# The opening of the first stage as one listed order for all engines

## The chip, the core and the metric

The kernel runs on one core of one Trainium2 chip. A core has five engines that take their instructions in order, each from a queue of its own: PE (TensorE, matrix products), ACT (ScalarE), DVE (VectorE), POOL (GpSimd) and SP (SyncE, which here only issues transfers). Sixteen DMA engines move data between HBM and the core. The metric is the device time of one execution in microseconds (us); a change is quoted against the kernel before.

## What is computed

```python
scores = q @ k.T / 8          # 4 sequences, 8 heads, 576 positions, head size 64
scores = where(0 <= i - j < 64, scores, -1e9)
x = softmax(scores) @ v       # joined over heads: 2304 tokens x 512
h = max(x @ w1, x @ w2, x @ w3)        # 512 -> 768
y = h @ w_out                          # 768 -> 512
h2 = y @ w_in                          # 512 -> 2048
g = where(h2 >= 1, h2, where(h2 <= -1, 0, (h2 + 1)**2 / 4))
out = g @ w_out2                       # 2048 -> 512
```

The weights arrive as 64-bit floats; q, k and v as 32-bit floats. Each big product is made of three passes over rounded "high" and "low" parts: high x high, high x low, low x high.

## The kernel before

**The first stage.** It interleaves the attention with the products of x with w1, w2 and w3. Attention is cut into 36 blocks `g` of 64 queries; two neighbouring blocks share one load of q and k. Tokens are cut into nine column blocks `j` of 256 (four attention blocks each). One *product* (`a_item`, 12 matmuls of 256 columns, line 423) multiplies one column block by one 128-column slice `f` of one of the three weights `w`; every column block takes 18 products. Products of blocks 0 and 1 are interleaved from the twelfth on (`LAG`), so in the order of issue the products A0 to A17 are fifteen of block 0 and three of block 1. After A17 come 144 more, and then two further stages (lines 766 and 993).

**An attention block, step by step.** `load` brings q and k (SP); `prep` transposes them on PE (line 296) and copies the results out of PSUM with ACT (`qt`, line 299) and DVE (`kring`, line 301); `qk` multiplies (PE, line 335); `red` takes the masked maximum (DVE, line 346); `ex` takes four exponentials (ACT, line 358); `norm` forms a reciprocal (DVE, lines 366 and 367) and scales the row (POOL, line 368); `ptr` transposes (PE, line 377); `ptc` copies out (line 385 on DVE for odd blocks below 8, else ACT); `pv` multiplies by v (PE, line 398); `val` writes the high part of x (ACT) and the low part (DVE, line 113).

**A weight pair, step by step.** The 18 weight slices are fetched and decoded as nine pairs of 1024 columns, pair n serving products 2n and 2n+1 of a column block. `w_load` issues two transfers of 512 KB into a staging buffer `wst`, of which there are three (`NW`). `w_word` decodes the upper and the lower words in place (two ACT instructions, lines 194 and 110). `w_shift` shifts the upper word into a tile `wt`, of which there are two (DVE, line 206). `w_add` adds the lower word (DVE, line 210). `w_high` rounds the sum into the arena (ACT, `arena<-wt`, line 110). `w_low` subtracts in two halves (POOL, line 113). So the five links are a chain: words, shift, add, high, low.

**What sets the order.** Steps are put at positions, a position being an index of a product, and sorted. `SEQ` (line 58) lists the steps of blocks 0 to 3 and three weight pairs ahead of the first product; blocks 4 to 7 lie at fixed distances from the products; a weight pair follows each product of column block 0. Up to position 12 (`visits[0]`) this is only the order in which steps are handed to a planner, which arranges each engine's queue by its own reckoning of times; from there on `chained` ties each step behind the ones before it on PE, ACT, DVE and SP. No tie makes one engine wait for another: it fixes the order in each queue.

**PSUM.** Products and the transposes of `prep` share one pool (`pmm`) of three buffers; a buffer comes free when its reader on ACT or DVE is done.

Of the kernel before, what the change touches and what calls it, by code (L numbers as in the profile page):

```python
# [58 lines left out]
    "L0 V1 P0 L2 V2 V3 Q0 Q1 E0 N0 E1 N1 P2 T0 Q2 X0 T1 Q3 E2 N2 E3 X1 N3 "  # L59
    "T2 X2 T3 X3 W3"  # L60
# [5 lines left out]
def kernel(ctx, tc, q, k, v, w1, w2, w3, wo1, wi2, wo2, out, hd, x2d, td, gd):  # L66
# [83 lines left out]
    queued = []  # L150

    def after_queued(fn, *args):
        with ExitStack() as stack:
            for i in queued:
                stack.enter_context(tc.issue_after(i))
            n = len(nc.cur_bb.bb.instructions)
            fn(*args)
        ends = [i for i in nc.cur_bb.bb.instructions[n:] if i.engine == mybir.EngineType.SP]
        queued[:] = ends[-1:] or queued

# [45 lines left out]
    def w_value(st):  # L212
        w_shift(st)
        w_add(st)

    def w_high(s, st):
        act_copy(s[:, 0], decoded[id(st)].bitcast(F32))

    def w_low(s, st):
        t = decoded.pop(id(st)).bitcast(F32)  # L220
        for x in (slice(0, 512), slice(512, 1024)):
            sub(nc.gpsimd, s[:, 1, x], t[:, x], f32(s[:, 0, x]))
# [18 lines left out]
    def load(g):  # L241
# [3 lines left out]
        if g in pet and g % 2 == 0:  # L245
            t = apool.tile([P, 2, 512], F32, tag="nat", name="nat", bufs=4)
            for x, src in enumerate((q, k)):
# [8 lines left out]
            nat[g // 2] = t  # L256
# [28 lines left out]

    def prep(g):
        b, i, s = blk(g)
        d = st_g[g]
        if g in pet:
            if g % 2:  # L290
                return
            qt = apool.tile([P, NP, 2, BL], F32, tag="qt2", name="qt2", bufs=2)
            for x in range(2):
                tp = pmm.tile([P, NP, P], F32, tag="mm", name="tp")
                for p in range(NP):
                    nc.tensor.transpose(tp[:, p, :], nat[g // 2][:, x, p * P:(p + 1) * P], ident)
                tp = tp.rearrange("a p (t c) -> a p t c", t=2)
                if x == 0:
                    act_copy(qt, tp)
                else:  # L300
                    nc.vector.tensor_copy(kring[:, :, s:s + 2, :], tp)
            for x in range(2):
                st_g[g + x]["q"] = qt[:, :, x, :]
# [76 lines left out]
    def ptc(g):  # L380
        d = st_g[g]
        W = d["W"]
        pt = apool.tile([P, NP, P], F32, tag="pt", name="pt", bufs=3)
        if g < 8 and g % 2:
            nc.vector.tensor_copy(pt[0:W], d["pps"][0:W])
        else:
            act_copy(pt[0:W], d["pps"][0:W])
        d["pt"] = pt
# [13 lines left out]
    def values(g, n, xt, off):  # L402
# [3 lines left out]
        act_copy(hl[0], o)  # L406
        sub(nc.vector, hl[1], o, f32(hl[0]))
# [9 lines left out]
    def a_item(j, f, w):  # L417
        t0, n = blocks1[j]
# [185 lines left out]
    def val(g, n=1):  # L604
        j, o = gblock[g]
        if o == 0:
            xt_new(j)
        values(g, n, xts[j], o)

    def pv_x(g):  # L610
        pv(g)
        val(g)

    def qk_r(g):
        qk(g)
        red(g)
# [8 lines left out]
    FS = (0, 3, 1, 4, 2, 5)  # L625
    order1 = [(w, f) for f in FS for w in range(3)]
# [443 lines left out]
```

## Time and profile before

| | us |
|---|---|
| median of 3 runs | 765.75 (765.6 to 770.11) |
| the profiled execution | 766.48 |
| its span, first to last instruction | 764.6 |
| PE busy | 738.2 (97%) |
| DVE, ACT, POOL busy | 574.2, 424.7, 261.9 |

The profiled execution is 0.73 us above the median, and 1.9 us of its time lie outside its span. Shares over the whole span say little about one stage: the page's 40 slices of 19.1 us each, and tables by stretch, show where PE isn't busy and at which clock it ran. A row of the timeline gives start, duration, engine, line, operation and tiles, with the idle time before it and what ended it in square brackets. A row of the groups gives the busy sum and the mean duration of one instruction.

### The profile page before, as it was taken

How to read it: one execution, taken by the hardware profiler on the slowest of the kernel's cores; microseconds unless marked ns; L12 is line 12 of the kernel's file. 1: busy time of each engine (PE TensorE's matmuls, PEld its weight loads, DVE VectorE, ACT ScalarE, POOL GpSimd, SP SyncE). 2: the span in 40 equal slices, each digit the busy share in tenths (PEclk: the TensorE clock that was granted, in tenths of full speed). 3: DMA queues.
4: the chain of work that ended last, by engine and by line, in shares of the span. 5: the costliest groups of instructions: out<-in, count | busy, mean ns of one | idle time of the engine just before them, and what ended most of it. 6: DMA issues, size and time to landing. Idle time of an engine off the chain costs nothing.

```text
span 764.6 us, 17458 instructions
## 1 busy us (share of the span) xinstructions
PE 738.2 (97%) x6680; PEld 718.2 (94%) x6680; DVE 574.2 (75%) x1313; ACT 424.7 (56%) x808; POOL 261.9 (34%) x315
## 2 busy tenths in 40 slices
PE   4798999999999999999999999999999999999997
PEld 3687989999999999999999999999999999999997
DVE  3697667777787884768876688777878999988881
ACT  5795575556565543535457767767675444443330
POOL 1647295355535462200048533731368000000000
PEclk9599999999999999999999999999999999999999
DMA  9977879896999975796778553555556545544421
GB/s 260 249 238 196 211 176 272 246 341 174 266 269 280 312 251 186 222 295 209 211 231 274 192 161 120 192 193 177 188 172 193 170 139 152 164 127 121 129 82 56
DMA packets 221651, 154.75 MB, mean 202 GB/s; under 512 B 95232, under 2 KB 213632, under 8 KB 221568
## 3 DMA queue, kind: packets, MB, share of 16 engines
q1 hardware_dynamic: 191600, 110.91, 52.0%
q10 hardware_dynamic: 26384, 28.06, 10.5%
q0 software_dynamic: 3584, 14.68, 4.9%
q8 instruction: 52, 0.85, 0.4%
q14 instruction: 31, 0.25, 0.1%
HBM read 98.24 MB, written 55.38 MB: 201 GB/s over the span
## 4 chain that ended last, share of the span: by engine, by line
PE 43%; DVE 3%; ACT 2%; DMA 1%; issue 1%; ACTq 0%; DVEq 0%
PE cc L766 6%; PE dz L993 6%; PE dx L993 6%; PE dy L993 6%; PE ce L766 6%; PE ca L766 6%; PE cb L766 3%; PE dw L993 3%; DVE plain L490 1%; DMA plain<-t_scratch 1%; ACT arena L110 1%; DVE side L113 1%; DMA plain<-g_scratch 1%; ACT ut L861 1%; DVE left L113 0%
## 5 line engine op out<-in xcount | busy, mean ns | idle before, releaser
L423 PE MATMUL ps<-xt,arena 128*128 128x256 f32 x1944 | 235.6, 281 | 5.0 <-ACT ht L110 1.7
L423 PEld LDWEIGHTS ps<-xt,arena 128*128 128x128 f32 x1944 | 229.5, 188 | 9.1 <-issue 2.0
L110 ACT ACTIVATE side<-plain 128x1024 fp32r<-128x1024 f32 (+3 forms) x64 | 61.6, 978 | 55.9 <-DVE plain L490 36.2
L110 ACT ACTIVATE arena<-plain 128x1024 fp32r<-128x1024 f32 (+3 forms) x62 | 60.0, 977 | 36.1 <-DVE plain L490 23.5
L490 DVE TENSOR_TENSOR plain<-plain 128x256 f32<-128x256 f32 (+1 forms) x172 | 76.3, 461 | 4.3 <-DMA plain<-g_scratch 1.9
L113 DVE TENSOR_TENSOR side<-plain,side 128x1024 fp32r<-128x1024 f32 (+3 forms) x53 | 60.8, 1172 | 17.7 <-ACT side L110 17.7
L113 POOL TENSOR_TENSOR arena<-plain,arena 128x256 fp32r<-128x256 f32 (+1 forms) x65 | 55.0, 879 | 47.3 <-ACT arena L110 47.2
L113 POOL TENSOR_TENSOR side<-plain,side 128x256 fp32r<-128x256 f32 (+1 forms) x38 | 34.6, 945 | 102.4 <-ACT side L110 83.6
L358 ACT ACTIVATE sm<-sm,nm 128x128 f32<-128x128 f32 (+1 forms) x144 | 55.3, 388 | 16.9 <-DVE nm L346 14.8
L110 ACT ACTIVATE ht<-ps 128x256 f32<-128x256 f32 x54 | 20.5, 382 | 79.2 <-PE ps L423 48.4
L368 POOL TENSOR_TENSOR sm<-sm,rs 128x512 f32<-128x512 f32 (+1 forms) x36 | 36.3, 1007 | 69.3 <-DVE rs L367 43.1
L490 DVE TENSOR_TENSOR hq<-hq 128x128 f32<-128x128 f32 x108 | 54.1, 502 | 1.6
L113 DVE TENSOR_TENSOR arena<-plain,arena 128x1024 fp32r<-128x1024 f32 (+3 forms) x34 | 40.7, 1202 | 6.0 <-ACT arena L110 5.8
L862 ACT ACTIVATE ut<-ut 128x288 f32<-128x288 f32 x64 | 43.9, 686 | 2.0
L436 DVE TENSOR_TENSOR ht<-ps,ht 128x256 f32<-128x256 f32 x54 | 22.7, 421 | 29.5 <-PE ps L423 14.9
L210 DVE CUSTOM_DVE_ANT_0 wt<-wst,wt 128x1024 uint16<-128x1024 uint16 (+1 forms) x47 | 42.1, 912 | 1.6 <-ACT wst L110 0.3
L871 DVE SCALAR_TENSOR_TENSOR ut<-ut,evt 128x864 f32<-128x864 f32 x32 | 38.3, 1196 | 1.6 <-ACT ut L862 1.6
L490 POOL TENSOR_TENSOR wx<-wt 128x256 f32<-128x256 f32 x26 | 19.3, 743 | 56.2 <-DVE wt L210 48.5
L436 DVE TENSOR_TENSOR hq<-ps,ht 128x256 f32<-128x256 f32 x54 | 22.5, 416 | 20.3 <-PE ps L423 17.4
L113 POOL TENSOR_TENSOR arena<-wt,arena 128x512 fp32r<-128x512 f32 (+1 forms) x26 | 33.9, 1330 | 9.0 <-ACT arena L110 8.9
L847 DVE TENSOR_TENSOR evt<-cc,evt 128x288 f32<-128x288 f32 x64 | 29.1, 455 | 8.8 <-PE cc L766 6.6
L110 ACT ACTIVATE evt<-ca 128x288 f32<-128x288 f32 x40 | 16.2, 406 | 34.0 <-PE ca L766 28.9
(164 smaller groups left out, 1775.9 us busy)
## 6 DMA issues: line engine op xcount, KB each, us to landing
g_scratch<-ut ACTq DMA_DIRECT2D x64, 288.0 KB, 3.0
plain<-g_scratch SPq DMA_DIRECT2D x36, 512.0 KB, 4.3
plain<-t_scratch SPq DMA_DIRECT2D x16, 896.0 KB, 5.2
h_scratch<-hq SPq DMA_DIRECT2D x27, 448.0 KB, 5.1
plain<-h_scratch SPq DMA_DIRECT2D x12, 1008.0 KB, 7.6
wst<-in_moe_w_out SPq DMA_DIRECT2D x22, 512.0 KB, 5.8
wst<-in_moe_w SPq DMA_DIRECT2D x18, 512.0 KB, 6.3
wst<-in_moe_w_in SPq DMA_DIRECT2D x16, 512.0 KB, 5.6
```

The lines of the kernel that those rows point to most:

```text
L110: nc.scalar.activation(dst, src, AF.Copy, scale=scale)
L113: eng.tensor_tensor(dst, a, b, op=ALU.subtract)
L210: nc.vector.tensor_tensor(t[:, x], t[:, x], st[:, x, 0], op=ALU.add)
L358: nc.scalar.activation(sm[:, p, 0:W], sm[:, p, 0:W], AF.Exp, bias=d["nm"][:, p:p + 1], scale=-1.0, accum_out=ss[:, p:p + 1])
L368: nc.gpsimd.tensor_tensor(sm[:, :, 0:W], sm[:, :, 0:W], rs.unsqueeze(2).to_broadcast([P, NP, W]), op=ALU.mult)
L423: nc.tensor.matmul(ps[:, 0:n], w_col((w, f), wl, kt), xt[:, xl, kt, 0:n], start=(x == 0), stop=(x == len(passes) - 1))
L436: nc.vector.tensor_tensor(t[:, 0:n], ps[:, 0:n], part[j, f][:, 0:n], op=ALU.max)
L490: eng.tensor_tensor(o, a, b, op=op)
L766: nc.tensor.matmul(o, wt.of(m, wl)[:, at * P:(at + 1) * P], wx.of(m, xl)[:, kt], start=start and x == 0, stop=x == len(passes) - 1, skip_g ...
L862: nc.scalar.activation(o, o, AF.Square)
L871: nc.vector.scalar_tensor_tensor(o, o, 2.0 ** WS, x, op0=ALU.min, op1=ALU.max)
L993: nc.tensor.matmul(o, quarter(gc[k % 4].hl[gl], RA[m])[:, r], wd[p].of(m, wl), start=bool(first and p == 0 and i == 0), stop=p == NPR - 1 ...
```

## The change

`SEQ` becomes one list of single steps up to the end of the eighteenth product, for all engines, the loads included. Each token is a step and a number: LQ, LK, LV, LW load q, k, v and a weight pair; TQ, TK and CQ, CK are the transposes and the copies of `prep`; QK, R, E as before, R and E in halves a and b; S is the reciprocal and N the scaling; PT, PC, PV as before; VH and VL the two parts of x; A the twelve matmuls of a product and D its read-out; H and ST sums and store of h; W1., W0., SH, AD, HI, LO the links of a weight pair. A star puts a copy on DVE (for CK: on ACT). Tokens without `@` stand ahead of A0; `@x` is a position.

All steps are now tied from the start, and POOL's too up to position 12. Blocks 4 to 7, and the steps of blocks 8 and 9 up to their scaling, leave the loops and stand in the list. The weight chain is rewired: the lower word is decoded into `wt` (`w_lower`), the upper word is shifted in place in `wst` (`w_upper`), `w_sum` adds them, and `w_high` rounds the shifted upper word alone, so that it no longer needs the sum. HI0, HI3 and HI8 run on DVE, the others on ACT. No instruction is added or left out; copies change engine and order. One step far behind, the last of eight steps on the second loaded chunk of the third stage, moves from position 31.58 to 31.05.

```diff
 SEQ = (
-    "L0 V1 P0 L2 V2 V3 Q0 Q1 E0 N0 E1 N1 P2 T0 Q2 X0 T1 Q3 E2 N2 E3 X1 N3 "
-    "T2 X2 T3 X3 W3"
+    "LQ0 LK0 TQ0 LQ1 CQ0 TK0 LK1 *CK0 TQ1 QK0 LK2 CQ1 QK1 R0a LQ2 TK1 E0a R0b R1a E0b TK2 LW0 CK1 E1a TQ2 S0 QK2 R1b "
+    "N0 CQ2 QK3 E1b R2a PT0 E2a R2b LV1 CK2 E2b *PC0 LV2 QK4 W0.0 S1 PV0 S2 LW1 N1 W1.0 R4a R3a N2 PT1 E3a R3b R4b "
+    "QK5 E3b SH0 E4b PT2 S3 LV3 *HI0 W0.1 AD0 LV4 W1.1 LQ3 *PC1 LO0a E4a *PC2 PV1 LK3 VH0 SH1 TQ3 N3 R5a LV5 HI1 TK3 "
+    "R5b LO0b S4 LW2 PT3 VH1 VL0 E5a VL1 PV2 N4 *PC3 CQ3 *CK3 AD1 PT4 VH2 E5b QK6 LQ4 VL2 LO1a W1.2 S5 PV3 R6a LW3 "
+    "W0.2 N5 TQ4 R6b QK7 E6a SH2 PT5 CQ4 LO1b R7a HI2 R7b LV6 AD2 E7a LW4 VH3 LO2a W1.3 VL3 "
+    "A0@0 E6b@0.19 SH3@0.33 E7b@0.74 LO2b@0.83 S6@0.9 A1@1 LW5@1.26 D0@1.29 S7@1.45 W1.4@1.56 N6@1.73 A2@2 PC4@2.33 "
+    "*HI3@2.47 W0.3@2.75 D1@2.98 N7@2.98 A3@3 D2@3.25 W0.4@3.3 LV7@3.3 AD3@3.42 PT6@3.58 W1.5@3.74 PV4@3.77 SH4@3.92 "
+    "A4@4 LW6@4.01 D3@4.32 *PC5@4.36 LO3a@4.36 PC6@4.59 A5@5 HI4@5.01 SH5@5.2 AD4@5.57 HI5@5.68 PT7@5.75 A6@6 "
+    "*PC7@6.21 LO3b@6.21 W1.6@6.23 LW7@6.31 D4@6.55 PV5@6.72 LO4a@6.86 D5@6.88 D6@6.92 A7@7 VH5@7.28 W0.5@7.55 "
+    "H5a@7.71 A8@8 LO4b@8.12 D7@8.24 LK4@8.25 W1.7@8.43 VL5@8.49 AD5@8.88 A9@9 W0.6@9.04 H5b@9.32 VH4@9.37 LW8@9.38 "
+    "TK4@9.44 D8@9.51 LO5a@9.51 D9@9.56 VL4@9.64 *CK4@9.71 PV6@9.83 SH6@9.91 A10@10 VH6@10.2 LO5b@10.2 HI6@10.4 "
+    "VL6@10.5 PV7@10.72 AD6@10.85 W1.8@10.94 A11@11 D10@11.36 W0.7@11.37 LO6a@11.43 QK8@11.54 D11@11.69 QK9@11.75 "
+    "VH7@11.78 R8a@11.89 A12@12 ST5@12 LO6b@12.01 VL7@12.1 E8a@12.24 R8b@12.39 E8b@12.84 SH7@12.9 A13@13 D12@13.39 "
+    "AD7@13.54 HI7@13.66 A14@14 H11a@14.4 D13@14.41 W0.8@14.68 LO7a@14.84 R9a@14.84 A15@15 R9b@15.29 E9a@15.44 "
+    "D14@15.6 LO7b@15.89 S8@15.9 E9b@15.98 A16@16 D15@16.28 H11b@16.79 A17@17 N8@17.23 D16@17.28 S9@17.58 SH8@17.96 "
+    "*HI8@17.98 AD8@17.98 D17@17.98 LO8a@17.98 LO8b@17.98 N9@17.98 ST11@18"
 )
...
+    def w_lower(st):
+        t = decoded[id(st)] = stg2.tile([P, 1024], I32, tag="wt", name="wt", bufs=WT)
+        act_copy(t, st[:, :, 0].bitcast(U32), scale=2.0 ** -29)
+
+    def w_upper(st):
+        w = st[:, :, 1]
+        nc.vector.tensor_scalar(w, w, 3, None, op0=ALU.logical_shift_left)
+
+    def w_sum(st):
+        t = decoded[id(st)]
+        nc.vector.tensor_tensor(t, t, st[:, :, 1], op=ALU.add)
+
+    def w_high(s, st, copy):
+        copy(s[:, 0], st[:, :, 1].bitcast(F32))
...
-    TIED = (mybir.EngineType.PE, mybir.EngineType.Activation, mybir.EngineType.DVE, mybir.EngineType.SP)
+    TIED = [mybir.EngineType.PE, mybir.EngineType.Activation, mybir.EngineType.DVE, mybir.EngineType.SP, mybir.EngineType.Pool]
     for at, _, fn, args in order:
         if fn:
-            chained(fn, *args, tie=at >= visits[0])
+            if at >= visits[0]:
+                TIED[4:] = ()
+            chained(fn, *args)
...
-                      (28.1, 28.11, 28.12, 28.13, 29.9, 30.05, 30.58, 31.58),
+                      (28.1, 28.11, 28.12, 28.13, 29.9, 30.05, 30.58, 31.05),
```

## Rows read from the trace of the kernel before

**Rows 1.** The page's slices of 19.1 us: PE's busy tenths and its granted clock.

```profile
PE   4798999999999999999999999999999999999997
PEclk9599999999999999999999999999999999999999
```

**Rows 2.** Table by stretch: length, then each engine's busy us; PEclk, DMA share, GB/s.

```profile
17.00:34.70 17.70, 11.68 (x104) 8.57 (x104) 12.86 (x35) 14.49 (x39) 11.08 (x9) 0.53 0.96 239
34.70:75.10 40.40, 36.64 (x381) 33.62 (x378) 33.68 (x88) 31.30 (x72) 23.91 (x17) 0.99 0.76 229
75.10:124.00 48.90, 47.83 (x517) 45.84 (x516) 32.55 (x111) 30.75 (x80) 27.72 (x34) 1.00 0.82 205
124.00:752.00 628.00, 624.59 (x5516) 615.80 (x5515) 486.76 (x1041) 339.70 (x594) 195.89 (x243) 1.00 0.66 201
```

**Rows 3.** Timeline: ACT's first copy, the first product, the eighteenth product's read-out.

```profile
5.14 0.60 ACT L110 ACTIVATE qt<-tp 128x512 f32<-128x512 f32 x1 [2.91 <-PE tp L296]
...
34.74 1.82 PEld L423 LDWEIGHTS ps<-xt,arena 128*128 128x128 f32 x13 [0.33 <-issue]
...
75.21 0.42 DVE L436 TENSOR_TENSOR hq<-ps,ht 128x256 f32<-128x256 f32 x1 [0.97 <-PE ps L423]
```

**Rows 4.** Waits from 0 to 80 us: total us, times, longest.

```profile
ACT arena L110 <- DVE wt L210: 7.8, 4, 4.2
PE ops L398 <- DVE xt L113: 5.6, 2, 4.3
...
PE ps L423 <- ACT ht L110: 1.7, 1, 1.7
```

**Rows 5.** Table by stretch again, one us each, around both changes of clock.

```profile
18.00:19.00 1.00, 0.00 (x0) 0.00 (x0) 1.00 (x3) 1.00 (x6) 0.00 (x0) 0.61 1.13 338
...
35.00:36.00 1.00, 1.00 (x8) 1.00 (x9) 1.00 (x8) 0.42 (x3) 0.59 (x1) 0.85 1.09 354
```

**Rows 6.** Groups by form, 0 to 73.7 us, ACT, DVE, POOL: busy us, mean ns.

```profile
L358 ACT ACTIVATE sm<-sm,nm 128x128 f32<-128x128 f32 x32 | 12.4, 390 | 2.8 <-DVE nm L346 1.5 <-POOL sm L368 1.4
L110 ACT ACTIVATE wst<-wst 128x1024 int32<-128x1024 uint32 x9 | 10.3, 1146 | 0.0
...
L110 ACT ACTIVATE arena<-wt 128x1024 fp32r<-128x1024 f32 x9 | 9.5, 1058 | 7.9 <-DVE wt L210 7.8
...
L110 ACT ACTIVATE qt<-tp 128x512 f32<-128x512 f32 x6 | 3.5, 587 | 2.9 <-PE tp L296 2.9
L110 ACT ACTIVATE xt<-ops 128x256 fp32r<-128x256 f32 x8 | 3.0, 370 | 0.0
...
L210 DVE CUSTOM_DVE_ANT_0 wt<-wst,wt 128x2048 uint16<-128x2048 uint16 x9 | 14.3, 1587 | 0.9 <-ACT wst L110 0.3
...
L113 POOL TENSOR_TENSOR arena<-wt,arena 128x512 fp32r<-128x512 f32 x18 | 27.8, 1568 | 9.0 <-ACT arena L110 8.9
```

**Rows 7.** Timeline of PE's weight loads, 76 to 89 us: one row for each kind.

```profile
76.31 0.87 PEld L377 LDWEIGHTS pps<-ident,sm 128*128 128x128 f32 x8
...
77.37 0.86 PEld L335 LDWEIGHTS sps<-kring,qt 64*64 64x64 f32 x32 [0.20 <-issue]
...
82.62 0.90 PEld L296 LDWEIGHTS tp<-ident,nat 128*128 128x128 f32 x8
...
83.48 4.27 PEld L423 LDWEIGHTS ps<-xt,arena 128*128 128x128 f32 x36
...
87.89 1.16 PEld L398 LDWEIGHTS ops<-pt,vr 128*64 128x64 f32 x32
```

**Rows 8.** Tile wst, 0 to 80 us: durations min/median/max in ns; landing of its transfers.

```profile
L206 DVE TENSOR_SCALAR wt<-wst x9: 681/694/1808, 16.2 to 64.0; 128x1024 int32<-128x1024 int32 x9
L210 DVE CUSTOM_DVE_ANT_0 wt<-wst,wt x9: 1216/1260/2300, 17.2 to 66.0; 128x2048 uint16<-128x2048 uint16 x9
...
DMA to landing us min/median/max: 3.5/6.3/10.0
```

**Rows 9.** Timeline of DVE: the step moved far behind.

```profile
577.04 1.52 DVE L113 TENSOR_TENSOR left<-plain,left 128x768 fp32r<-128x768 f32 x1
```

More of the change, by code (lines that the diff above doesn't have):

```diff
@@ L1 @@
+import re
 from collections import defaultdict
@@ L149 @@
     wslot = {}
[L150 to L159, printed above, removed]
     def w_load(pair, slot):
@@ L239, in natural, with load @@
         return g % 4 != 0
-    def load(g):
+    def load(g, half=(0, 1)):
         b, i, s = blk(g)
@@ L245, in load @@
         if g in pet and g % 2 == 0:
-            t = apool.tile([P, 2, 512], F32, tag="nat", name="nat", bufs=4)
-            for x, src in enumerate((q, k)):
+            if g // 2 not in nat:
+                nat[g // 2] = apool.tile([P, 2, 512], F32, tag="nat", name="nat", bufs=4)
+            t = nat[g // 2]
+            for x in half:
+                src = (q, k)[x]
                 for y in range(1) if i + 1 < NBB else range(2):
@@ L284, in vload, with prep_t, prep_c @@
         d["vr"] = t
+    def prep_t(g, x):
+        tp = st_g[g]["tp", x] = pmm.tile([P, NP, P], F32, tag="mm", name="tp")
+        for p in range(NP):
+            nc.tensor.transpose(tp[:, p, :], nat[g // 2][:, x, p * P:(p + 1) * P], ident)
+    def prep_c(g, x, copy):
+        tp = st_g[g]["tp", x].rearrange("a p (t c) -> a p t c", t=2)
+        if x == 0:
+            qt = apool.tile([P, NP, 2, BL], F32, tag="qt2", name="qt2", bufs=2)
+            copy(qt, tp)
+            for y in range(2):
+                st_g[g + y]["q"] = qt[:, :, y, :]
+        else:
+            copy(kring[:, :, blk(g)[2]:blk(g)[2] + 2, :], tp)
     def prep(g):
@@ L291, in prep @@
                 return
-            qt = apool.tile([P, NP, 2, BL], F32, tag="qt2", name="qt2", bufs=2)
             for x in range(2):
[L294 to L303, printed above, removed]
+                prep_t(g, x)
+                prep_c(g, x, (act_copy, nc.vector.tensor_copy)[x])
         else:
@@ L353, in ex @@
         W, sm = d["W"], d["sm"]
-        if pairs[0] == 0:
+        if "ss" not in d:
             d["ss"] = apool.tile([P, NP], F32, tag="ss", name="ss", bufs=5)
@@ L378, in ptr, with ptc @@
         d["pps"] = pps
-    def ptc(g):
+    def ptc(g, copy=act_copy):
         d = st_g[g]
@@ L383, in ptc @@
         pt = apool.tile([P, NP, P], F32, tag="pt", name="pt", bufs=3)
[L384 to L387, printed above, removed]
+        copy(pt[0:W], d["pps"][0:W])
         d["pt"] = pt
@@ L683 @@
+    for x, tok in enumerate(SEQ.split()):
+        tok, _, at = tok.partition("@")
+        for step in early(tok):
+            put(float(at or -100 + 0.01 * x), *step)
     g0 = blocks1[PB][0] // BL
```

131 lines of the change are left out of this document (61 added, 70 removed).

## Prediction, made before the changed kernel ran

> **What bounds the kernel now.** I read the page's slices first, to see where PE isn't full or not at its clock. From the third slice on PE is at nine tenths and the clock full; the first two slices are at four and seven tenths, with half the clock in the second [rows 1]. So whatever this change can give lies ahead of about 80 us. The table by stretch confirms it: from 124 to 752 us PE is busy 624.6 of 628 us, and just behind the eighteenth product 47.8 of 48.9 [rows 2]. What the opening saves should therefore reach the end, since the stretches behind it are bound by PE and move forward as a whole.
>
> Then the timeline, for two marks. The first product starts at 34.74. A17 ends at about 75.1, since its read-out on DVE starts at 75.21 released by PE [rows 3]. Up to A17 the list issues the same work as the kernel before (I counted each kind of step to that mark: five pairs of transposes plus block 10's, ten QK, eight PT, eight PV), so the gain of the opening is 75.1 less the new end of A17.
>
> The waits say who held whom. ACT waited 7.8 us in four waits for the sum on DVE before it could round a weight's high part: the link that the change takes out. PE waited once 4.3 us for the low part of x on DVE [rows 4]. [...]
>
> **What A0 costs to reach.** The list doesn't shorten the work ahead of A0; it even adds to it (E5 whole, halves of E6 and E7, QK6, QK7, PT4, PT5, the transposes of block 8). A0 needs VL3 on DVE, and that needs VH3 on ACT. ACT's share of the list ahead of and with VH3, by mean durations [rows 6]: 28 exponentials at 0.39 (10.9; block 0's are narrower, which I ignore), six word decodes at 1.15 (6.9), HI1 and HI2 at 1.06 (2.1), seven copies of transposes at 0.59 (4.1), four VH at 0.37 (1.5): 25.5 us. ACT's first copy starts at 5.14 [rows 3], so VH3 can't end before 30.6, and A0 not before 31. Walking the list step by step with these durations I find three waits that stay: ACT idles about 1.8 us ahead of 12 us, while the first loads, transposes and copies still follow one another; 1.0 at HI1, which stands behind SH1 and so behind AD0 on DVE; 0.4 at VH2, behind PV2. That gives 34.2: the first product starts where it did, not earlier. Bounds: 32 (two thirds of these 3.2 us gone) and 37 (the list's PE steps on the chain at half clock, some ten of them ahead of A0, each 0.3 longer).
>
> **What lies between A0 and A17.** Work that PE does there, from weight loads in the stage behind, at full clock [rows 7]: 18 products at 4.27/3 = 1.42 (25.6); PT6 and PT7 0.9; PV4 to PV7 2.3; QK8 and QK9 0.9; TK4 and the transposes of block 10 1.35; some three quarters of a us for switches at 0.1 to 0.2 each: 31.8. Before, the same stretch took 75.1 - 34.7 = 40.4, since it held 2.2 us more of attention on PE (two PT, two QK, half of a pair of transposes, at the same rows) and 3.8 us in which PE wasn't busy [rows 2]; the other 2.6 are short pieces between bursts, which the view counts as busy.
>
> Then the waits that the new order makes. (a) TK4 stands ahead of A10 on PE and needs LK4, which SP issues behind LW7; LW7 waits for the buffer that HI4 and AD4 free (my walk: 44.4), and behind load 10 (0.5 MB) come 1 MB and 0.25 MB, some 1.8 MB at the stretch's 229 GB/s [rows 2], 7.9 us: about 52 where PE comes to it at 51: 1.0 us. PV6, A10 and all later products are queued behind TK4. (b) The transposes of block 10 lie between A15 and A16, while D14 and D15 are listed behind them; with three PSUM buffers the second transpose must wait for the first copy and A16 for the second or for D15: two copies near 0.6 [rows 6], 1.3 us. (c) Weight pairs that come just in time (LO3 to LO5 end 0.3 to 3 us ahead of their product in the walk): 1.0 us. Sum 34.2 + 31.8 + 1.0 + 1.3 + 1.0 = 69.3. Unknown from the trace: whether (a) is 0 or, with the longest landing of 10.0 us instead of the median of 6.3 [rows 8], 5; I take 1.0, since the queue is as full as before.
>
> **The smaller edits.** Rounding high beside the sum removes ACT's 7.8 us of waits for DVE [rows 4] and costs nothing on DVE: shift and sum are the same instructions. Cover is lost at one place: the lower word now goes to one of two `wt` tiles, so ACT stands behind POOL's lows of two pairs before; in the walk they are 0.5 to 3 us early; where they aren't, the next exponentials and read-outs on ACT wait too. On POOL the list only orders lows and scalings, and POOL was busy 23.9 of 40.4 us [rows 2]; on SP it puts the first weight pair ahead of v, which ACT, full by then, doesn't see. The in-place shift and the HI copies on DVE have no row. Between 0.68, the shortest shift, and 1.81, the longest [rows 8], I take 1.0; DVE was free for 6.7 of 40.4 us behind A0 [rows 2], so both ends stay hidden there; not so HI0, which puts up to 0.8 us on A0's chain and is in its bounds. The spread 681 to 1808 ns comes where POOL's lows run beside the shift. [...]
>
> The step moved far behind: 1.52 us of DVE ahead of read-outs that PE waits for in tenths [rows 9]. Moved before them it can save or cost a few tenths; I count 0, with 0.5 to either side.
>
> **Sum.** 75.1 - 69.3 = 5.8 us. The profiled execution took 766.48, so 760.7; it stood 0.73 above the median of 765.75, so 760.0 for the median.
>
> **Rivals.**
> *The first half packs tighter.* If the list's order matches the chip, ACT's waits ahead of 12 us shrink and DVE's work overlaps: A0 at 32 and 0.7 us of waits behind it: 32 + 31.8 + 0.7 = 64.5, gain 10.6, 755.2. For it: ACT was busy only 14.5 of 17.7 us ahead of A0 and DVE 12.9 [rows 2]. Against it: ACT's 25.5 us can't start sooner.
> *The loads set the pace (slower side).* SP's queue is now one fixed order with three staging buffers; a weight load that waits for its buffer holds LK4, and so PE at TK4. If a pair comes every 4.5 us LK4 is in time within 1 us. From LK4 landing later than 57 the gain is gone; with landings near 10 us for three loads in a row (3 x 3.7 us late) it lands at 63, and A17 ends at 80.3: 771.0. For it: landings up to 10.0 us occurred [rows 8]. Against it: the median is 6.3, and the list starts loads as soon as the planner did.
> *The clock.* PE has done PT5 some 3 us before A0 in the walk, a gap near the one behind which the clock fell (4.3 us, [rows 4, 5]). [...] Against it: the gap is shorter than the one seen.
>
> **How the numbers follow.** About 1% (7.7 us) is what a measurement of this kernel can tell from no change. Forecast (a gain of 3 to 7.7): 0.45. Tighter packing (above 7.7): 0.30. The clock (1 to 3): 0.10. The loads: 0.15, of it 0.05 with landings later still (A17 behind 82.8, slower by over 1%) and 0.10 within. So faster 0.30, same 0.65, slower 0.05. The likeliest time is 760.0; its own range is 757 to 763. The range for 8 in 10 runs from 754 (A0 at 32, no waits: 63.8, 11.3 gained) to 767 (A0 at 37 with 6 us of waits: 74.8, or the milder cases of the loads).
>
> **What would show it.** [...] I am wrong in A0's term if it starts before 32 or after 37; in the waits if PE stands for over 2 us at `tp` for `nat<-in_k`, or at `ps`; and in the carry-over if A17 ends sooner and the span doesn't shrink by as much.

## The result, and the profile after

The changed kernel takes 772.83 us (770.35 to 774.74, seven runs) beside 765.75 for the kernel before (764.07 to 770.33): the ratio is 1.0056, with a 95% interval from 1.0029 to 1.0083. The two medians lie further apart, 0.92%; the median of the kernel before in four later sets of rounds was 767.35 to 768.93, so 765.75, from which the forecast starts, is a low one. Forecast were 760.0 and a range to 767. The profiled execution took 770.42, its span 768.6.

The page's slices of 19.1 us, PE's busy tenths and its granted clock, answer [rows 1]. PE is no busier in the first two slices together (5 and 6 tenths for 4 and 7), but its clock is higher in the second. The third slice is less full (8 for 9); the fourth is fuller (9 for 8) at a lower clock. The fourteenth, 249 to 268 us, stands at 8 where the kernel before has 9:

```profile
PE   5689999999999899999999999999999999999997
PEclk9798999999999999999999999999999999999999
```

The table by stretch answers [rows 2] (length, each engine's busy us, PEclk, DMA share, GB/s). Ahead of A0 the clock is now 0.80 and not 0.53; between A0 and A17 it is 0.88 and not 0.99, and that stretch has grown from 40.4 to 41.6 us:

```profile
17.00:34.40 17.40, 9.66 (x110) 7.38 (x108) 13.72 (x43) 14.31 (x42) 9.17 (x8) 0.80 1.10 265
34.40:76.00 41.60, 37.05 (x333) 34.71 (x334) 28.15 (x61) 26.62 (x54) 19.06 (x15) 0.88 0.66 193
...
124.00:752.00 628.00, 622.46 (x5491) 614.15 (x5490) 488.10 (x1042) 340.17 (x595) 195.88 (x244) 1.00 0.67 202
```

PE's timeline from 28 to 82 us shows where (start, length, line, operation, count, and in brackets the idle time ahead with what ended it; L285 transposes, L401 PV, L433 products):

```profile
34.43 7.72 PE L433 MATMUL ps<-xt,arena 128*128 128x256 f32 x48 [2.94 <-ACT xt L125]
...
48.63 4.51 PE L433 MATMUL ps<-xt,arena 128*128 128x256 f32 x36
55.32 1.09 PE L285 MATMUL tp<-ident,nat 128*128 128x128 f32 x4 [2.18 <-DMA nat<-in_k]
57.20 1.12 PE L401 MATMUL ops<-pt,vr 128*64 128x64 f32 x16 [0.80 <-DVE xt L128]
58.25 2.93 PE L433 MATMUL ps<-xt,arena 128*128 128x256 f32 x12
61.11 1.12 PE L401 MATMUL ops<-pt,vr 128*64 128x64 f32 x16
62.17 1.66 PE L433 MATMUL ps<-xt,arena 128*128 128x256 f32 x12
...
64.59 5.86 PE L433 MATMUL ps<-xt,arena 128*128 128x256 f32 x48
70.29 0.60 PE L285 MATMUL tp<-ident,nat 128*128 128x128 f32 x4
71.58 0.66 PE L285 MATMUL tp<-ident,nat 128*128 128x128 f32 x4 [0.69 <-ACT qt L125]
73.02 4.47 PE L433 MATMUL ps<-xt,arena 128*128 128x256 f32 x36 [0.78 <-DVE kring L295]
```

The first product starts at 34.43. Four products take 7.72 us there and 5.86 at 64.59. PE stands at TK4, the transposes of the keys of pair 4, and at PV6, and A10 behind them takes 2.93 us where A11 takes 1.66. The granted clock by stretches of 4 us says why:

```profile
32.00:36.00 4.00, 1.49 (x6) 1.29 (x7) 2.56 (x9) 4.00 (x12) 2.27 (x2) 0.85 1.10 315
36.00:40.00 4.00, 4.00 (x27) 4.00 (x27) 2.29 (x7) 3.29 (x10) 2.82 (x3) 0.72 0.98 282
40.00:44.00 4.00, 4.00 (x46) 3.77 (x45) 3.21 (x5) 4.00 (x6) 1.58 (x1) 1.00 0.05 14
...
56.00:60.00 4.00, 3.21 (x26) 2.69 (x26) 2.24 (x4) 3.07 (x7) 0.00 (x0) 0.50 1.16 306
60.00:64.00 4.00, 4.00 (x42) 3.53 (x45) 0.90 (x3) 2.33 (x3) 2.52 (x2) 0.73 0.92 250
```

A17 is the second of the three products from 73.02 on: it ends at 73.02 + 2/3 of 4.47, or 76.0, 0.9 later than before. The waits from 0 to 80 us answer [rows 4]. ACT's 7.8 us for `wt` are gone, as meant; its waits for the weights' transfers have grown from 2.8 us to 7.3, the longest of them 3.89 us at the word step W1.7, and ACT issues VH4, which PV6 needs, behind it:

```profile
ACT wst L185 <- DMA wst<-in_moe_w: 7.3, 3, 3.9
...
ACT arena L125 <- DVE wst L205: 0.5, 2, 0.2
```

ACT's timeline at that step, with VH4 as its last row:

```profile
54.28 1.11 ACT L185 ACTIVATE wst<-wst 128x1024 f32<-128x1024 f32 x1 [3.89 <-DMA wst<-in_moe_w]
...
56.33 0.36 ACT L125 ACTIVATE xt<-ops 128x256 fp32r<-128x256 f32 x1
```

On SP's queue the loads come in bursts: nothing moves from 40 to 44 us (14 GB/s above), since the next weight pair waits for its buffer, and the pair LW7 at 46.96 stands ahead of the keys LK4 at 48.02:

```profile
46.96 1.02 SPq L170 DMA_DIRECT2D wst<-in_moe_w  x2
48.02 1.88 SPq L249 DMA_DIRECT2D nat<-in_k  x2
```

LW7 is issued when DVE ends the sum AD4, which frees its buffer:

```profile
44.57 2.33 DVE L209 CUSTOM_DVE_ANT_0 wt<-wst,wt 128x2048 uint16<-128x2048 uint16 x1
```

The larger part of the loss in this trace lies where nothing was changed. PE's longest wait behind 76 us stands near 250 us and is 3.5 us long, with a fall of the clock behind it (0.82 granted from 252 to 254 us, 0.50 from 254 to 256); in the trace of the kernel before the same wait was 0.9 us. The row of PE's waits from 76 to 400 us in the changed kernel:

```profile
PE ps L433 <- DVE hq L450: 3.5, 1, 3.5
```

And the same row of the kernel before:

```profile
PE ps L423 <- DVE hq L436: 0.9, 1, 0.9
```

To put the parts beside each other I use the starts of DVE's 108 read-outs of products in the first stage, in their order. The 13th is the first behind A17's. From the 13th to the 72nd nearly every trace needs 160.4 to 160.5 us, from the 81st to the 108th 64.0 (e_warm and the runs with moved stores below are the exceptions); what differs is the start of the 13th, the piece from the 72nd to the 81st (called the loose stretch below, about 242 to 270 us), and what follows the 108th. For the two profiled executions: 81.58 and 82.51; 24.38 and 28.42; 434.19 and 433.26. So 0.9 lost in the opening, 4.0 in the loose stretch, 0.9 regained at the end: 764.6 + 4.0 = 768.6.

### The profile page after: what moved, and what is told of

It reads as the page before. It is cut to its first block, busy times and chain, and to the rows that moved or that the text cites. A ratio compares the mean times of both kernels' runs of the same rounds, so it can differ in the third digit from the quotient of the medians.

```text
span 768.6 us, 17450 instructions
## 1 busy us (share of the span) xinstructions
PE 738.3 (96%) x6680; PEld 720.6 (94%) x6680; DVE 574.6 (75%) x1315; ACT 423.3 (55%) x806; POOL 258.2 (34%) x315
## 5 line engine op out<-in xcount | busy, mean ns | idle before, releaser
L433 PE MATMUL ps<-xt,arena 128*128 128x256 f32 x1944 | 239.2, 284 | 8.3 <-DVE hq L450 3.5
L433 PEld LDWEIGHTS ps<-xt,arena 128*128 128x128 f32 x1944 | 233.3, 191 | 12.3 <-DVE hq L450 3.8
L185 ACT ACTIVATE wst<-wst 128x1024 f32<-128x1024 f32 x28 | 32.1, 1147 | 14.1 <-DMA wst<-in_moe_w 7.3
L128 POOL TENSOR_TENSOR arena<-wt,arena 128x512 fp32r<-128x512 f32 (+1 forms) x26 | 29.8, 1168 | 27.3 <-DVE wt L209 19.9
L504 POOL TENSOR_TENSOR wx<-wt 128x256 f32<-128x256 f32 x26 | 19.2, 740 | 57.7 <-DVE wt L197 50.0
```

What stands on the lines that cost most here:

```text
L128: eng.tensor_tensor(dst, a, b, op=ALU.subtract)
L185: nc.scalar.activation(w.bitcast(F32), w.bitcast(F32), AF.Prelu, scale=2.0 ** (WS - 119), alpha=2.0 ** 32)
L433: nc.tensor.matmul(ps[:, 0:n], w_col((w, f), wl, kt), xt[:, xl, kt, 0:n], start=(x == 0), stop=(x == len(passes) - 1))
L504: eng.tensor_tensor(o, a, b, op=op)
```

## The experiments

The first runs were to tell three readings apart. W: in the opening ACT's wait for a weight pair counts, not the keys' load alone. S: the longer wait near 250 us is a consequence of the change, by way of the loads held back (SP stood 14.5 us at the store ST11, so that the loads behind it came 5 us late). V: that wait differs from one execution to the next.

**The changed kernel once more** (r_after; no edit).

> The changed kernel once more, for a second trace. Theory S (the stop at 250 us has its cause in the opening: store ST11 held SP's queue for 14.5 us, and the loads behind it stay late): PE again waits over 2 us for a read-out near 250 us, and the time is 770 to 774. Theory V (that stop comes and goes with the speed of the transfers from run to run): the wait near 250 us is another one, under 1.5 us or in another place, with the opening as before (first product at 34.4, the eighteenth's end at 76).

773.33 us, 1.0078 [1.0054, 1.0102]. The 13th read-out at 82.49, the loose stretch 28.49, the wait 3.6 us: the same as the first trace. Between these two S holds and V doesn't.

**Keys of pair 4 sooner** (e_lk4):

```
- ... LK4@8.25 ...
+ ... LK4@3.95 A4@4 LW6@4.01 ...
```

> LK4 alone moved from behind LW7 to ahead of LW6. [...] Theory W (ACT's standing for the eighth weight pair, 3.9 us, is the cause, and it holds VH4 and with it PV6): TK4 runs earlier, but PE then stands at PV6 until about 57, so A17 ends within 1 us of 76 and the time changes by less than 1 us.

770.06 us, 1.0028 [1.0003, 1.0052]. TK4 no longer waits, but PE then stands at PV6, which needs block 4's value and so VH4 behind ACT's word step:

```profile
53.91 0.60 PE L285 MATMUL tp<-ident,nat 128*128 128x128 f32 x4
57.69 1.12 PE L401 MATMUL ops<-pt,vr 128*64 128x64 f32 x16 [3.17 <-DVE xt L128]
58.74 2.73 PE L433 MATMUL ps<-xt,arena 128*128 128x256 f32 x12
```

The 13th read-out comes at 82.37, 0.1 sooner. Two waits of nearly one length stood behind each other, and only one was taken out. The time is another matter: 770.06 us stands beside 773.33 of the changed kernel in the same rounds (r_after), 3.3 lower with intervals that just don't overlap, where W had less than 1. So most of what this load is worth doesn't lie in the opening; the trace of this run, with a loose stretch of 29.37, doesn't show it.

**The keys, and block 4's value ahead of the word step** (e_lk4_vh4):

```
+ LK4@3.95 A4@4 ... VH4@6.95 VL4@6.96 A7@7
- LK4@8.25 ... VH4@9.37 ... VL4@9.64
```

> LK4 ahead of LW6 as in the run before, and VH4 and VL4 moved ahead of the decode of the eighth pair on ACT and DVE. Theory W: now neither the load nor ACT's wait for the eighth pair stands between A9 and A11, so PE goes on at full clock; A17 ends near 71 to 72, the time falls by 4 to 5 us against the changed kernel. [...] A third way: the weight pairs themselves come too late (A10 waits for LO5a, A12 for LO6a); then A17 gains under 2 us whatever is moved.

766.57 us, 0.9998 [0.9967, 1.0030]. The stands at TK4 and PV6 are gone (0.37 us is left at A10 and 0.94 at PV7), and with them the second fall of the clock (granted 1.00 from 52 to 64 us): A10 takes 1.68 us.

```profile
54.86 0.60 PE L285 MATMUL tp<-ident,nat 128*128 128x128 f32 x4
55.39 0.69 PE L401 MATMUL ops<-pt,vr 128*64 128x64 f32 x16
56.44 1.68 PE L433 MATMUL ps<-xt,arena 128*128 128x256 f32 x12 [0.37 <-DVE hq L450]
```

The 13th read-out starts at 80.05, 2.5 us sooner than in the changed kernel, although the first product came 1.3 us later in this trace. W holds for the opening. The time is 6.8 us below r_after, where W had 4 to 5, and the loose stretch of this trace is 1.7 us shorter than r_after's.

**The first column's sums stored sooner** (e_st11):

```
- ... H11b@16.79 ... ST11@18
+ ... D13@14.41 H11b@14.45 ST11@14.5 ...
```

> H11b and ST11 alone moved to 14.45 and 14.5, so that SP's queue isn't held behind the second sum. Theory S: loads behind the store start some 5 us earlier against PE, the wait near 250 us goes, the eighteenth product stays at 76, and the time falls by 3 to 4 us. Theory V: the loads start earlier, but by 190 us they stand where they stood anyway, and the time changes by less than 1.5 us.

772.52 us, 1.0075 [1.0047, 1.0103]. The loads behind the store start in time, and the loose stretch is 28.58 us as before: the held store isn't the cause, and S in that form falls (it had 3 to 4 us; the time is 0.8 below r_after).

**The kernel before, traced again** (r_before; no edit). Two new theories of the loose stretch: D, it is how far the transfers lag behind the walk there; O, the changed order put it there.

> The kernel before, traced a second time. Its times spread from 764.4 to 771.1 us in the runs so far and fall into two heaps, about 764 to 766 and 767 to 771. Theory D (the stretch from 190 to 250 us is paced by transfers, and the wait of TensorE near 250 us for DVE's hq read-out is how late a weight pair of the second stage lands): the wait is there in this kernel too, at a size that changes from run to run, between 0 and 4 us; a span of 766 us or more goes with a wait of 2 us or more and with a lower granted clock behind it, a span of 763 to 764.6 with one of at most 1 us. Theory O (the wait is put there by the changed order of the opening): 0.9 us as in the first trace, whatever the span.

768.48 us, 1.0009 [0.9977, 1.0042]. In this trace the wait is 4.5 us, the loose stretch 30.40 and the span 770.3, with the 13th read-out at 81.50: the same kernel, and a longer stretch than any of the changed one's up to then. O in that form falls: the wait is no work of the changed order alone. SP's rows show what differs; the program is the same, and DVE's 72nd read-out stands at 242.09 and 242.03. The first trace of the kernel before:

```profile
240.71 0.57 SPq L443 DMA_DIRECT2D h_scratch<-hq  x1
...
245.92 4.49 SPq L171 DMA_DIRECT2D wst<-in_moe_w_out  x2
```

The second trace of it:

```profile
243.29 0.56 SPq L443 DMA_DIRECT2D h_scratch<-hq  x1
...
250.79 2.49 SPq L171 DMA_DIRECT2D wst<-in_moe_w_out  x2
```

The store was issued 2.6 us later, and what waits for it came 3.5 us later. That is DVE's read-out into `hq`, of which there are three buffers; the store frees one. DVE's row of the first trace:

```profile
249.46 0.42 DVE L436 TENSOR_TENSOR hq<-ps,ht 128x256 f32<-128x256 f32 x1 [2.84 <-DMA h_scratch<-hq]
```

And that of the second:

```profile
253.00 0.42 DVE L436 TENSOR_TENSOR hq<-ps,ht 128x256 f32<-128x256 f32 x1 [6.43 <-DMA h_scratch<-hq]
```

The transfers are close to full there. The DMA view from 190 to 245 us (packets, bytes, rate) of the first trace:

```profile
DMA packets 24731, 14.57 MB, mean 265 GB/s; under 512 B 18656, under 2 KB 22560, under 8 KB 24723
```

And of the second:

```profile
DMA packets 24342, 14.20 MB, mean 258 GB/s; under 512 B 18640, under 2 KB 22224, under 8 KB 24333
```

The share of the DMA engines from 190 to 245 us was 0.94 in the first and 0.90 in the second; 0.37 MB fewer, at 265 GB/s, are 1.4 us. Why the second moved less at a lower share isn't shown. Three quarters of the packets are under 512 bytes. In the first trace the engines give 265 GB/s at a share of 0.94 here, while from 255 to 260 us, with 430 of 1801 packets under 512 bytes, they give 363 at a share of 1.09.

**The second stage's weight pairs loaded sooner** (e_slot in the changed kernel, b_slot in the one before):

```
- SLOT = dict(load=-4, ...
+ SLOT = dict(load=-7, ...
```

> The changed kernel with one number changed: the loads of the second stage's weight pairs are put 7 places of the walk ahead of their slot, not 4, so that they are issued some 3 us sooner. Theory D: ACT's wait for the pair near 249 us, 3.9 us in the changed kernel, falls below 1.5; TensorE's wait near 250 us falls from 3.5 to at most 1, the granted clock in 252 to 258 us stays at 1.00, and the time falls by 3 to 4 us, to 769 to 770. Theory O: the wait stays at 3 us or more and the time at 772 to 774.

> The kernel before with the same one number changed (loads of the second stage's pairs 7 places ahead, not 4). Theory D: the upper of the two heaps of its times goes, median 764 to 765 beside 767 for the kernel before in the same rounds. Theory O: nothing to gain here but the 0.9 us of its first trace, median 766 to 768 with the same spread.

772.22 us (1.0079 [1.0045, 1.0112]) and 769.5 (1.0034 [1.0003, 1.0065]). ACT's wait for the pair near 249 us fell from 3.9 to 1.9 us in e_slot, but PE's wait stayed at 3.1: the pair's landing wasn't what PE waited for. In b_slot the wait was gone in the trace (loose stretch 23.21), and the median still no better. My form of D, by way of the weight pair, falls; the transfers' lag stays. The times of the two runs say less of it than the traces. In e_slot's the 13th read-out comes at 86.03, 3.5 later than in the changed kernel, of which 2.5 arise ahead of the first moved load (the first product starts at 35.75, and the first four take 8.88 us); in b_slot's the part behind the 108th took 436.2 us, 2.4 more than the mean of the kernel before.

**The stores 3 places sooner** (e_sto4 in the changed kernel, b_sto4 in the one before, e_best3 with the opening mended as in e_best below). Theory H: the landing of the store is the wait. D': the lag is there whatever stands first.

```
- put(at + 7, h_store, args[0], args[1] - 3)
+ put(at + 4, h_store, args[0], args[1] - 3)
```

> The changed kernel with the finished sums of the walk stored 3 places sooner (4 places behind the last product of their column, not 7), so that SP asks for each store ahead of some raw loads rather than behind them. Theory H (the wait near 250 us is the landing of one such store, which frees the third hq buffer for DVE's next read-out; it is late because it stands in SP's queue behind raw loads in a stretch where the transfers have no room): the time from the 72nd to the 81st of DVE's read-outs, 28.4 us in the changed kernel and 24.4 to 30.4 in the two traces of the kernel before, falls to 23 to 24, the wait to at most 0.5, the granted clock there stays at 1.00, and the time falls by 4 to 5 us to 768 to 769. Theory D' (the transfers are behind the walk there whatever stands first): the wait moves to another transfer, 27 us or more, 771 to 774.

> The kernel before with the same stores 3 places sooner. Theory H: the upper heap of its times goes, 763 to 765 for all runs and a median 2 to 4 below the kernel before in the same rounds. Theory D': the two heaps stay, median 766 to 769.

> The changed kernel with the opening mended (keys of pair 4 ahead, block 4's value split ahead of the waiting word step, sums of the first column stored at the 14.5th place, the two read-outs ahead of block 10's transposes; its walk ran 3.1 us ahead of the kernel before in the trace with these edits) and the stores 3 places sooner. Theory H: the 3 us of the opening are kept over the wait near 250 us: 759.5 to 762. Theory D': lost there, 766 to 768.

779.58 us (1.0182 [1.0132, 1.0232]), 772.93 (1.0075 [1.0041, 1.0110]) and 771.06 (1.0038 [1.0007, 1.0068]). H was right on the link: in b_sto4 no wait of PE is left between 240 and 260 us, and the loose stretch is 23.20. But the stores now stand on SP ahead of their data: between 90 and 232 us SP waits 11.4 us for `hq` sums in b_sto4, the longest 6.8. What is queued behind them came later, and PE stands between 215 and 225 us in the three traces, again for a buffer of `hq`; the way from the 13th to the 72nd read-out grew from 160.5 to 167.8 (b_sto4), 168.1 (e_best3) and 168.9 (e_sto4). D' was nearer on the time, but all three runs are 3 to 6 us slower than it had. PE's longest waits from 100 to 400 us in e_sto4:

```profile
PE ps L433 <- DVE hq L450: 3.4, 1, 3.4
PE ps L433 <- ACT ht L125: 2.3, 1, 2.3
```

**Work in the gap ahead of the first product** (e_warm; block 5's transposes again, into the same tile):

```
+ def again(g):
+     for _ in range(6):
+         for p in range(NP):
+             nc.tensor.transpose(d["pps"][0:d["W"], p, :], d["sm"][:, p, 0:d["W"]], ident)
- SH2 PT5 CQ4
+ SH2 PT5 XP5 CQ4
```

> The changed kernel with block 5's transposes repeated six times into the same tile ahead of the first product: work for TensorE in the 2.9 us in which it stands for xt. If the standing is what lowers its clock there: granted clock 1.00 in 32 to 40 us, the first four products 5.7 to 6.0 us, not 7.7, the read-out of the eighteenth product about 1.9 us sooner. If the clock falls for another reason: 0.85 and 0.72 there as in the changed kernel and no product sooner. The time over the whole: down by 0 to 2 us, since the wait near 250 us takes up what comes sooner.

770.03 us, 1.0030 [1.0001, 1.0059]. The clock stays full, and the four products take 6.21 us, not 7.72:

```profile
32.00:36.00 4.00, 3.81 (x32) 3.37 (x31) 2.74 (x12) 4.00 (x12) 1.73 (x2) 1.00 1.15 311
36.00:40.00 4.00, 4.00 (x36) 4.00 (x36) 3.11 (x8) 2.93 (x11) 2.99 (x3) 1.00 0.96 287
```

So it was the standing that lowered the clock; 6.21, not the 5.7 to 6.0 of the expectation, is what the four products need there at full clock. The next wait swallows the gain: TK4 starts at 54.98 instead of 55.32, since LK4 comes no sooner, and the 13th read-out at 82.14 instead of 82.51. The ratio of 1.0030 is lower than the changed kernel's, but the intervals overlap, and this trace is the longer one: 771.4 us, with 161.46 from the 13th to the 72nd read-out and 29.50 in the loose stretch. So no gain in the time is shown.

**The weights' new wiring alone** (b_wire; kernel before, order left to the planner):

```
- w_words(st); w_value(st); w_high(s, st); w_low(s, st)
+ w_word(st, 1)
+ act_copy(t, st[:, :, 0].bitcast(U32), scale=2.0 ** -29)
+ nc.vector.tensor_scalar(w, w, 3, None, op0=ALU.logical_shift_left)
+ nc.vector.tensor_tensor(t, t, w, op=ALU.add)
+ act_copy(s[:, 0], w.bitcast(F32))
+ w_low(s, st)
```

> The kernel before, its order still the planner's, with the new wiring of the weights alone (low word decoded into a tile of its own, shift in place, high part rounded from the shifted word, so that it no longer stands behind the addition). ACT's four waits for wt ahead of arena, 7.8 us in the kernel before, are gone. If the wiring is worth something by itself: the 13th read-out 1 to 3 us sooner than the 81.5 us of the kernel before, and a median 1 to 2 us lower. If what is gained there only moves to the next wait (loads, PSUM buffers): 81 to 82 us and no difference in the median.

768.58 us beside 768.93, 0.9978 [0.9945, 1.0010]. ACT's waits for `wt` ahead of `arena` are gone, but ACT now waits 4.9 us for the weights' transfers from 0 to 80 us and 5.3 for products on PE (2.8 and 2.9 in the kernel before), and PE's longest wait (4.3 us for the low part of x, [rows 4]) is as long as it was. The 13th read-out is at 80.84, where four traces of the kernel before have 80.50 to 81.73.

**Two more traces of each kernel** (r_after2, r_after3, r_before2, r_before3; no edits).

> The changed kernel, another trace. If the 5 us of the medians lie in the opening: the 13th of DVE's read-outs later than 83.5 us (82.5 in the two traces so far) and the stretch from the 72nd to the 81st 24 to 29 us. If they lie in the stretch paced by transfers: the 13th read-out at 82.3 to 82.8 again, and the stretch 28 to 31.

> As the run beside it: a 13th read-out later than 83.5 us speaks for the opening, one at 82.3 to 82.8 with a stretch of 28 to 31 us behind the 72nd for the transfers.

> The kernel before, another trace. If its two heaps of times are the two sizes of the stretch between the 72nd and the 81st read-out: an execution of 763 to 766 us has 23 to 25 us there, one of 768 to 772 has 28 to 31, and the 13th read-out is at 81.5 in both. If the heaps are the opening's: the 13th read-out differs by 3 us or more.

> As the run beside it: 763 to 766 us with 23 to 25 us in the stretch, 768 to 772 with 28 to 31, the 13th read-out at 81.5 in either.

With the traces above, in us (the last two columns are the issue of the store that frees the buffer, counted from the start of the 72nd read-out, and the time from there to the read-out that waits for it):

| kernel | 13th read-out | loose stretch | PE's wait in it | behind the 108th | span | store | to read-out |
|---|---|---|---|---|---|---|---|
| before | 81.58 | 24.38 | 0.9 | 434.19 | 764.63 | -1.38 | 8.75 |
| r_before | 81.50 | 30.40 | 4.5 | 433.87 | 770.28 | 1.26 | 9.71 |
| r_before2 | 81.73 | 27.93 | 2.9 | 433.29 | 767.39 | -0.49 | 9.86 |
| r_before3 | 80.50 | 25.40 | 1.9 | 433.66 | 763.98 | -0.66 | 9.02 |
| after | 82.51 | 28.42 | 3.5 | 433.26 | 768.64 | 0.22 | 9.71 |
| r_after | 82.49 | 28.49 | 3.6 | 434.84 | 770.32 | 0.50 | 9.58 |
| r_after2 | 83.33 | 30.09 | 3.9 | 433.07 | 770.93 | 1.42 | 9.00 |
| r_after3 | 83.62 | 29.74 | 3.5 | 433.26 | 771.04 | 0.51 | 9.48 |
| e_lk4_vh4 | 80.05 | 26.77 | 3.3 | 433.91 | 765.22 | -0.22 | 9.95 |
| b_wire | 80.84 | 27.71 | 2.7 | 434.24 | 767.22 | -0.70 | 9.86 |
| e_top | 77.49 | 25.87 | 2.4 | 433.72 | 761.59 | -0.61 | 9.49 |

The means of the four and four: the opening 81.33 and 82.99 (1.7 us lost), the loose stretch 27.03 and 29.19 (2.2 lost), the spans 766.6 and 770.2. Both guesses of these runs held in part: the opening ends later in two executions than in the two traced first, and the stretch is the larger item. Four traces with stretches from 24.4 to 30.4 don't fix a mean to better than about 1 us, and the last two of each kernel were taken on different chips. The stretch itself is 23.5 us and PE's wait where the clock holds at 1.00 (0.9, 1.9, 2.4 and 3.3 give 24.4, 25.4, 25.9 and 26.8), and 1.4 to 2.7 more in the others (granted from 250 to 255 and from 255 to 260 us: 0.83 and 0.83 in the changed kernel, 0.70 and 0.62 in r_before). The kernel before has both sorts of execution, with spans of 764 and of 767 to 770; all four traces of the changed one are of the longer sort, and none of its 19 executions is below 770.3 us. What the last columns add: from the store's issue to the read-out it is 8.8 to 10.0 us in all of them, and in the changed kernel the store is issued behind the 72nd read-out every time, in the kernel before ahead of it three times of four. So SP's queue is later against the walk. Why it should be always so isn't settled: the edits are in the opening and in one tail step, and neither an earlier walk (e_best below: 78.75, and a stretch of 29.38) nor the held store decides it. The keys of pair 4, loaded sooner, do part of it (e_lk4), by a path that no run shows.

**The mended order** (e_best, and e_top as the best version). e_best has the edits of e_lk4_vh4 and e_st11, D14 and D15 ahead of block 10's transposes, and the loads of e_slot; e_top has the work of e_warm in place of the loads:

```
- ... A15@15 ... D14@15.6 ... D15@16.28 ...
+ ... A15@15 D14@15.05 D15@15.1 ...
```

> The changed kernel with all that the runs point to: keys of block pair 4 loaded ahead of the seventh weight pair, block 4's value split ahead of the word step that waits for its transfer, the finished sums stored at the 14.5th place, the two read-outs ahead of block 10's transposes, and the second stage's pairs loaded 3 places sooner. If the losses add up: about 2.5 us in the opening, 1.3 at the transposes and 3 to 4 near 250 us less than the changed kernel, so 764 to 766 beside 773, and 1 to 3 us below the kernel before. If the stretch from 190 to 250 us is paced by transfers whatever the opening does (Theory D), the opening's part, about 3.8 us, is lost there again: 768 to 770.

> The changed kernel with the four mended places of the order (keys of pair 4 and block 4's value sooner, sums of the first column stored at the 14.5th place, the two read-outs ahead of block 10's transposes) and block 5's transposes repeated ahead of the first product. From the traces: 3.1 us ahead of the kernel before at the 13th read-out with the four places, 1.5 more with the clock kept, so 77 us there (81.5 before). Of these 4.5 us the stretch paced by transfers takes back what it takes in most executions (2 to 6 us in traces): median 763 to 766 beside 767 to 768, the fastest executions at 759 to 760.

e_best: 766.60 us, 0.9980 [0.9948, 1.0012], with single runs down to 759.94. e_top: 765.74 us beside 768.93, 0.9960 [0.9938, 0.9981], 0.4% below the kernel before, clear of the noise, though within the 1% that the prediction called no change. Two single executions of the changed kernel in the same rounds took 772.75 and 772.82. No run came to the 759 to 760 of the expectation; the lowest is 763.04. Its clock is 1.00 from A0 to A17, and TK4, PV6 and A10 follow with 0.84 us of standing (0.93 more at PV7):

```profile
34.81 6.21 PE L439 MATMUL ps<-xt,arena 128*128 128x256 f32 x48 [0.16 <-ACT xt L125]
...
52.43 0.60 PE L285 MATMUL tp<-ident,nat 128*128 128x128 f32 x4
52.96 0.69 PE L407 MATMUL ops<-pt,vr 128*64 128x64 f32 x16
54.49 1.68 PE L439 MATMUL ps<-xt,arena 128*128 128x256 f32 x12 [0.84 <-DVE hq L456]
...
67.99 4.47 PE L439 MATMUL ps<-xt,arena 128*128 128x256 f32 x36
```

A17 ends at 67.99 + 2.98 = 71.0, 5.0 us sooner than in the changed kernel and 1.7 behind the 69.3 of the forecast.

## Why the prediction was wrong

**A0's number was right, in part by luck.** 34.2 forecast, 34.43 in the trace. Between its first copy and VH3 ACT waited 5.1 us where the walk had 3.2: 1.3 at VH2 where it had 0.4, 1.5 at W1.2 for a transfer that the term had at nothing, and 0.2 at HI1 where it had 1.0. ACT's work up to VH3 came to 24.2 us and not 25.5, so the errors nearly cancel. The two longer waits, from 4 to 34.4 us:

```profile
ACT wst L185 <- DMA wst<-in_moe_w: 1.5, 1, 1.5
ACT xt L125 <- PE ops L401: 1.3, 1, 1.3
```

In the other three traces of the changed kernel the first product starts at 34.55, 35.34 and 36.56, still within the term's bounds of 32 to 37.

**The waits between A0 and A17 were sized too small, and the clock was left out of their sum.** This is the step that failed first. Forecast were 31.8 us of work and 3.3 of waits, to 69.3; it came to 76.0, 6.7 later. A0 accounts for 0.2. PE stands 2.18 at TK4 and 0.80 at PV6 where term (a) had 1.0; 0.69 + 0.78 = 1.5 at block 10's transposes where (b) had 1.3; nothing for a weight pair where (c) had 1.0: 4.45 in all, 1.15 more. The clock costs 7.72 - 6.21 = 1.5 at the first four products (6.21 is what e_warm needs with the clock kept) and 0.5 + 2 x 0.4 + 1.3 = 2.6 at TK4, PV6, PV7 and A10: 4.1. The last 1.2 is work that I had counted too short: the prediction itself finds 2.6 us of short pieces between bursts in the same stretch of the kernel before, and carries none of them into its sum. So the largest term is one that I had as a rival of its own at 0.10, with the argument that the gap ahead of A0 was shorter than the one of [rows 4, 5]; a gap of 2.94 us was enough, and e_warm shows that filling it keeps the clock. The chances give that rival a gain of 1 to 3 us; no run of the changed kernel shows it: in this trace the clock costs 4.1 us and the opening ends 0.9 later. This first fall isn't in every execution: in r_after3 the clock fell further ahead and was back at 1.00 from 36 us on, so that the four products took 6.21 us there too, and A17 still came later, with 3.20 us at TK4:

```profile
36.56 6.21 PE L433 MATMUL ps<-xt,arena 128*128 128x256 f32 x48 [1.58 <-ACT xt L125]
```

The clock and the loads came as one thing, and I had set them apart as two: the second fall (granted 0.50 from 56 to 60 us) came behind the stand at TK4, and with the stands at TK4 and PV6 gone it was gone too (e_lk4_vh4).

**The place was seen, the size not.** I had named TK4 behind LK4 behind LW7 and put PE there at 51 us; it came at 53 and stood until 55.3. Most of that is the buffer and not the transfers: SP issued LW7 at 46.96, right behind AD4, where my walk had 44.4, and the keys were there 8.4 us later, where term (a) had 7.9. In e_warm, with the clock kept, LW7 comes at 47.17, so this isn't the clock's doing. What I also missed is that LK4 wasn't the only thing late. The weight pair W1.7 landed at 54.3, ACT held VH4 behind it, and with the keys in time PV6 stood to 57.7 all the same (e_lk4). In a list that binds every engine, a late transfer holds all that is listed behind its first reader, as VH4 here.

**The gain of the wiring.** The 7.8 us of ACT's waits were real and went away, and b_wire shows them worth nothing that can be told from zero: ACT then waited for transfers and for PE instead.

**Carry-over was wrong.** I read "busy 624.6 of 628 us" [rows 2] as a kernel bound by PE that moves forward as a whole. In the eight traces of the two kernels the walk does so to 0.1 us everywhere but in one place: for some 55 us ahead of 245 the transfers are at a share of 0.90 to 0.95, and how late SP issues one store against the walk, with 8.8 to 9.9 us for its landing, decides how long PE stands near 250. In the one trace that I had, that wait was 0.9 us. It was a lucky execution: three more have 4.5, 2.9 and 1.9. For the profiled execution the parts add up: 760.7 forecast, 6.7 in the opening, 4.0 in the loose stretch, 0.9 regained at the end, 770.5 beside 770.42. Without the loose stretch the loss would be the opening's 0.9 to 1.7, within the 1% that I called no change.

**The smaller edits.** The step moved far behind starts at 578.83 and takes 1.51 us [rows 9]; behind the 108th read-out the four traces of each kernel need 433.8 and 433.6 us on average: 0, as forecast. The in-place shift took 680 to 1543 ns and the rounding on DVE 662 to 986, where I had taken 1.0 us. POOL's lows shrank, from 1.57 us on average [rows 6] to 1.34. The cause isn't shown; my guess is that fewer of them ran beside DVE's shifts. The one pair clearly above 1.3 us each, 3.39 from 42.42 on, runs beside two shifts and a sum of DVE, and of these the second shift took 1.20 us and the sum 2.33 where 0.68 and 1.21 are the shortest. In the kernel before, two of the four long shifts ran beside lows and two beside POOL's scalings, not all beside lows as I had read it.

**The chances, and two readings.** Nothing was wrong in kind with the rival of the slower side, but I let it end at a stall of one load and gave 0.05 to a loss over 1%. The measured loss is 0.56% (0.78% in r_after), within the 0.65 that I gave to no change, while the time, 772.83, lies outside the range. In that rival the gain is gone from a landing at 57.8 on by its own sum (52 + 5.8), not 57. And PE wasn't at nine tenths from the third slice on in the kernel before: its fourth slice has eight [rows 1].

## What to carry to other kernels

Before a gain at the start is carried to the end, look behind it for the stretch in which the transfers are full (here a share of 0.90 to 0.95), and trace the kernel before more than once: a wait of 0.9 us that is 4.5 in the next execution is a term of the sum, with both ends. When PE will stand for 2 to 4 us, price the clock with the stand, here 1.4 us on top in the changed kernel (0.83 granted from 250 to 260 us) and 2.4 in r_before (0.70, then 0.62). A wait that is taken out is worth only what the next one behind it leaves: here, at the end of the opening, the keys' load alone was worth 0.1 us and the clock 0.4, since each time the next transfer ended last, and the wiring nothing that can be told from zero; keys, block 4's value, the two read-outs and the clock together were worth 5.0 us at A17's end (e_top). And look at the time as well as at the place that was mended: the keys' load took 3.3 us off the median of the same rounds.

## What the runs showed of the hardware that I hadn't expected

One program, with its walk equal to 0.1 us, moved 14.57 and 14.20 MB in the same 55 us, and DVE's read-out stood until 8.8 and 9.7 us behind the issue of the store that frees its buffer. The length of a stand alone doesn't tell whether the clock falls: it held at 1.00 behind stands of 2.4 and 3.3 us in the loose stretch (e_top, e_lk4_vh4) and fell behind ones of 3.5 and 4.5 (the changed kernel's first trace and r_before: 0.83 and 0.70 from 250 to 255 us), behind the 2.94 us ahead of A0 (0.70 from 34 to 36 us), and behind 2.25 us ahead of 31.84 in r_after3 (granted clock 0.98 from 30 to 32 us, 0.50 from 32 to 34). Behind stands of 2.7 and 2.9 us (b_wire, r_before2) the loose stretch took 1.5 us more than 23.5 and the wait.
